# A linear-attention and dense block on one core: 14 additions and two subtractions made by accumulating transfers, query parts in two, and a new order of parts

## The chip, the cores and the metric

The kernel runs on one core of one Trainium2 chip. The metric is the device time of one execution in microseconds. A core has five engines that each take their own instructions in order: TensorE (PE in the profile; its weight loads are PEld), VectorE (DVE), ScalarE (ACT), GpSimd (POOL) and SyncE (SP), which here issues nearly all transfers. Engines wait for each other by semaphores. Transfers run on 16 transfer engines that all queues share.

## The reference

For 2048 tokens `x` of 512 features, a layer norm, a linear attention with 32 heads of 16 features, and a dense pair with Mish between give the output `x + s * g`:

```python
xn = _layernorm(x, axis=-1)
# attention: q, k, v from xn @ wqkv; pq, pk = q, k times w_phi per head
phi_q = jnp.concatenate([_softmax(pq, axis=-1), _softmax(-pq, axis=-1)], axis=-1)
phi_k = jnp.concatenate([_softmax(pk, axis=-1), _softmax(-pk, axis=-1)], axis=-1)
kv = jnp.einsum("bhsf,bhsd->bhfd", phi_k, v)
z  = jnp.einsum("bhsf->bhf", phi_k)
num = jnp.einsum("bhqf,bhfd->bhqd", phi_q, kv)
den = jnp.einsum("bhqf,bhf->bhq", phi_q, z)[..., None] + 1e-6
s = (num / den) @ wo                      # heads side by side
# dense: h = xn @ w1 + b1, mish(h) @ w2
g = _silu(_B_ref(xn, B_w1, B_b1, B_w2))
return x + s * g
```

What the change touches is `z`, the sum of the key maps over all tokens, and `wo`.

## The kernel before

Products keep float32 accuracy by halves: each operand is held as a high half (a rounded copy) and a low half (the value minus the high half), and a product is three matmuls, low x high, high x low and high x high. Large products go by a Strassen-like scheme of seven products of sums instead of eight. So ScalarE makes high halves (`split`, first line), and VectorE or GpSimd the sums and low halves (`either`: whichever the planner picks).

The work is written as some 200 parts, which `ORDER` lists by name, and each part issues operations into a `Program`:

- `wv`, `kh`, `kl`, `kd`, `ks`, `k2`, `k4`, `wq`, `wQ`: loads, sums and halves of the key, value and query weights; `b1` the bias.
- `N0` to `N15` (`norm`): load of 128 tokens, layer norm, transposes, sums and halves of the transposed block.
- `Ka`, `Kb`, `Kc`, `Kd` of token pair c: the seven key and value products of 256 tokens (tiles `kx`, `ky`, `kz`), their evacuation, and `k_soft`, the two softmaxes of a token block into `k0e` to `k15e`. `Kd` has one product, of whose result the map of the even block is made: `Kd6` makes `k12e`.
- `A0` to `A7` (`kv_acc`): the maps of a pair are added to the running sum `zacc` (128 x 1024, 512 KB), and every second time the products `kvp` of maps and values are issued.
- `z` (`sums`): the halves `zacch`, `zaccl` of `zacc`, its product with ones (`pz`), copied into `zb`; the block-diagonal form of `kvp`.
- `Q0` to `Q7` (`q_proj`): seven query products of 256 tokens (`qx`, `qy`, `qz`, six matmuls with 256 columns each) and the query softmaxes; `D0` to `D15` (`den`): the denominators, with `zb`.
- `Fa`, `Fb`, `Fc`, `Fd` of n (`ffn1a` to `ffn1d`): the first dense layer, two products, two, two and one of six matmuls with 512 columns (`fx`, `fy`, `fz`); results are spilled to HBM (`hd`). `P` makes weight halves (`w1ah`, `w1al`, `w1sh`, `w1sl`) and spills them, `M` loads them again (`w1b`).
- `Ua`, `Ub` (`num_a`, `num_b`): numerators; `O` (`att_out`): product with `wo`, spilled. `wo0`, `wo1` (`weights_o`): loads and halves of `wo`.
- `R`, `G` (`ffn2`), `E`, `H`: the second dense layer, SiLU and output.

TensorE executes its products in the order of the list, without exception. All else is ordered by a planner (`Program.simulate`): a list scheduler that plays the program through with a cost per operation (`cost`), a due time per operation that follows from where the TensorE work stands that needs it (changed by the entries of `SHIFT`, "part:operation:nanoseconds"), a pool of tiles, and a model of the transfers. It gives each operation an engine and a place. `locks` keeps VectorE's and GpSimd's operations on SBUF apart in the plan. The engines then run what was planned, each in its order, and wait where data isn't there.

Nearly every instruction is recorded by one line of `issue` (L404 in the profile), so the profile is read by tile names.

Of the kernel before, what the change touches and what calls it, by code (L numbers as in the profile page):

```python
# [48 lines left out]
SHIFT = """
kd:0:-9100 wv1:0:-1100 N1:2:-15000 N1:3:300 N1:5:5800 N1:13:4300 N1:14:-7000 kl:3:-10000 Ka2:3:-9700 N5:6:-2200  # L50
N5:8:-1200 N5:11:13000 N2:0:-3500 N2:2:-2000 N3:4:1500 N3:13:-11400 Kc0:7:4900 Kc0:10:14200 k4:0:-6900 Kd0:6:300
N6:14:-6700 P0:1:4800 P0:5:3800 P0:11:5000 Kb1:3:300 N7:6:-2800 N7:8:7300 N7:9:-6400 N8:8:-2700 N9:13:3600 Kc1:8:1800
Kd1:4:-7300 N10:3:-300 N11:0:5800 P4:0:-7000 P4:4:300 P4:5:3100 N14:8:-6800 Kd3:1:-5000 Kd3:6:-6400 A2:0:-3600
N13:5:-2500 Fa4:1:-1100 Fa4:3:3600 N15:4:10800 N15:6:-5000 N15:11:-300 Kc5:6:4400 Ka6:1:-600 Kc6:5:-300 Kc6:6:2600
P6:6:-1100 P6:8:5100 P3:3:-2600 P3:11:-2000 Kb7:1:2800 Fa3:1:-300 Fa3:3:300 P2:4:-2000 P2:6:1100 P2:10:800 Kd6:6:-8800
Kd6:9:-9500 Fb6:3:-2300 Fc3:1:1600 Fc3:2:800 Fc3:4:7900 wQ:1:2300 wQ:13:6600 Fa2:3:300 Fa2:4:-1900 Fa1:3:900
M4:1:-1400 P5:10:3200 Q0:7:14700 Q0:23:-2000 z:4:1200 z:5:11100 D0:0:800 D0:4:4700 D0:8:-800 L:5:-4200 L:9:-3000
D1:2:-8100 Q1:16:800 Q1:19:300 Q2:3:-15000 Q2:9:-2500 Q2:15:300 Q2:25:-1900 Q3:17:-4300 Q3:18:4700 Fc5:5:9400
D3:7:1800 D4:3:-4000 D4:4:6800 D4:5:1300 D4:6:11900 D4:10:11500 D5:1:-300 Fb11:1:-4700 Q4:7:-600 Q4:16:600 Q4:18:7800
Q4:20:800 Q4:21:-1400 Q4:23:-8800 Q5:25:-600 M3:1:-5000 M3:2:-6700 Fa12:1:800 D6:6:-500 D6:10:300 Fb10:1:-500  # L60
D7:1:5000 D7:4:6600 D8:1:-2400 D8:4:-500 D8:10:1400 Q6:1:4700 D9:10:800 Q7:1:7800 Q7:16:-4700 Q7:20:4800 Q7:21:-13000
Q7:23:-12900 M2:2:-5000 D10:6:-800 M6:2:-4100 D11:1:-1700 Ua0:1:-1100 Ua0:12:-800 Fc9:1:3400 D12:5:-5000 D13:0:-4400
D13:4:12500 Fa13:4:800 Ub0:14:-4300 wo0:1:-4500 Fc13:4:-13100 Fc7:2:15000 R0:8:4700 D14:6:-7800 O3:2:-900 Ua1:2:-4200
Ua1:4:-6700 Ua1:6:-3100 Ua1:11:-5000 Ua1:13:-300 Ua1:14:300 O5:2:-500 Fd13:2:-4200 O6:1:-2200 Ub1:5:-5000 Ub1:6:-2000
Ub1:8:-4500 G7:4:-2000 R2:0:-2200 R1:1:15000 R1:6:4200 R1:10:5800 G8:3:-5000 G8:6:1900 O11:2:-2000 R6:1:4900 R3:2:1600
R3:8:-3300 R4:1:2000 G11:0:-6800 G12:5:3100 G12:6:-1200 G13:5:-1100 G32:3:6500 G34:6:4000 G1:4:-15000 G3:0:5000
G4:0:-4100 G5:5:4000 G35:3:9300 G35:4:-5800 G35:6:3100 G14:0:-10200 G14:3:4000 E0:6:-2600 G15:2:800 G39:6:-300
G16:4:-5000 G41:3:1700 E5:4:-300 G20:0:800 G20:2:-2000 G20:3:-5300 G20:6:-5000 G42:3:5100 G42:5:-300 G43:2:4200
G44:2:300 G44:4:-2000 H4:2:1300 G46:3:6600 G46:6:300 G24:6:500 G47:5:-3000 G26:4:-1600 E6:2:-800 G49:0:-5000
G49:2:4000 G49:6:-1100 G49:9:2000 G49:12:-2200 G49:19:2200 G49:26:5000 G49:31:800 G49:36:2800 G49:42:-4700 G49:43:800  # L70
E7:9:-300 E7:10:15000 H3:7:2300 H6:8:800
"""
ACT_SET = {AF.Exp: 1, AF.Silu: 3, AF.Mish: 2}

# [5 lines left out]
class Program:  # L80
# [141 lines left out]
    def simulate(self, at):  # L222
# [49 lines left out]
        def go(o, e):  # L272
# [124 lines left out]
    def issue(self, tc):  # L397
        first, held = True, None
        for o in self.order():
            for i, (m, a, k) in enumerate(o.impl[o.eng][1]):  # L400

                e = self.eng["A" if first and m == "dma_start" else o.eng]
                first = first and m != "dma_start"
                ins = getattr(e, m)(*a, **k)  # L404
# [47 lines left out]
def block_kernel(ctx: ExitStack, tc: tile.TileContext, x, wqkT, wv, phi, wo, w1, b1, w2, out):  # L452
# [228 lines left out]
    def plus(t, ps):  # L681
        V.tensor_tensor(t, t, ps, op=ALU.add)
# [72 lines left out]
    def kv_d(c):  # L755
# [36 lines left out]
    def kv_acc(p):  # L792
# [379 lines left out]
    def sums():  # L1172
# [20 lines left out]
        for i in range(4):  # L1193
# [46 lines left out]
```

## Time and profile before

| what | value |
|---|---|
| median of 2 runs | 489.16 us (488.93 to 489.39) |
| profiled execution, span from first to last instruction | 488.7 us |
| granted TensorE clock | 1.000 |
| TensorE busy | 480.2 us |
| VectorE, ScalarE, GpSimd busy | 446.2, 293.4, 267.2 us |
| bytes moved by transfers | 105.70 MB, mean 216 GB/s |

The span is what the trace covers; the runs' time has some tenths of a microsecond around it. A busy time counts an engine once, however many of its instructions overlap. The page's rows by slices, each a fortieth of the span (12.2 us), give the busy share in tenths (9 is 90% or more):

```profile
PE   8899999999999999999999999999999999999996
DVE  6999999988899999999999899889989889999894
ACT  3997545654556453635345545677879687777631
POOL 3989998998490446798987686370021024120030
DMA  8812923968867689982959635726465646578172
```

Rows of a transfer give, from left to right, target and source, the issuing queue, the count, KB each and the median time from issue to landing. Rows of a tile give the shortest, median and longest duration in ns, and the first and last start in us. Rows of waits give who waited for whom, the total in us, how often, and the longest.

### The profile page before, as it was taken

To read this page: it belongs to the slowest core of one execution; us is meant where nothing else is said; L and a number is where in the kernel's file an instruction comes from. 1 tells how busy PE (TensorE), PEld (TensorE's weight loads), DVE (VectorE), ACT (ScalarE), POOL (GpSimd) and SP (SyncE) were. 2 spreads that over 40 slices of the span, in tenths; PEclk is the share of its full clock that TensorE was granted. 3 is DMA by queue.
4 is the path that set the end of the run, shared out by engine and by line. 5 is a ranking of instruction groups with operands and counts; after the bars stand their busy time and mean duration, and the time that the engine had idled before them with its cause. 6 is when DMAs were issued, how large, how long until landed. Compare 5 with 4: busy or idle time off the path is not lost.

```text
span 488.7 us, 10325 instructions
## 1 busy us (share of the span) xinstructions
PE 480.2 (98%) x3820; PEld 426.2 (87%) x3820; DVE 446.2 (91%) x893; ACT 293.4 (60%) x453; POOL 267.2 (55%) x197
## 2 busy tenths in 40 slices
PE   8899999999999999999999999999999999999996
PEld 7788888888887889898887878788899999999996
DVE  6999999988899999999999899889989889999894
ACT  3997545654556453635345545677879687777631
POOL 3989998998490446798987686370021024120030
PEclk9999999999999999999999999999999999999999
DMA  8812923968867689982959635726465646578172
GB/s 294 265 48 109 332 99 122 312 197 272 315 217 313 225 301 345 394 300 87 310 199 341 229 115 211 261 85 207 141 193 165 201 154 211 194 234 269 44 250 94
DMA packets 68641, 105.70 MB, mean 216 GB/s; under 512 B 6896, under 2 KB 37744, under 8 KB 68592
## 3 DMA queue, kind: packets, MB, share of 16 engines
q1 hardware_dynamic: 68448, 104.79, 62.9%
q8 instruction: 30, 0.49, 0.4%
q10 hardware_dynamic: 144, 0.26, 0.2%
q14 instruction: 19, 0.16, 0.1%
HBM read 60.60 MB, written 44.43 MB: 215 GB/s over the span
## 4 chain that ended last, share of the span: by engine, by line
PE 81%; DVE 8%; DMA 5%; issue 2%; ACT 1%; SPq 1%; POOL 1%; DVEq 0%; ACTq 0%
PE y L404 20%; PE fx L404 14%; PE pw L404 9%; PE kx L404 7%; PE fy L404 7%; PE qx L404 5%; PE ky L404 3%; PE fz L404 3%; PE qy L404 2%; PE kj L404 2%; PE pn L404 2%; PE kz L404 2%; DVE al L404 2%; DMA wvr<-wv 1%; DMA w1a<-w 1%
## 5 line engine op out<-in xcount | busy, mean ns | idle before, releaser
L404 POOL TENSOR_TENSOR al<-r,ah 128x896 fp32r<-128x896 f32 x8 | 17.0, 2130 | 87.4 <-DMA r<-hd 35.1
L404 ACT ACTIVATE ah<-r 128x896 fp32r<-128x896 f32 x56 | 50.9, 944 | 16.0 <-DVE r L404 12.9
L404 DVE TENSOR_TENSOR al<-r,ah 128x896 fp32r<-128x896 f32 x48 | 54.8, 1171 | 5.0 <-ACT ah L404 3.2
L404 DVE TENSOR_TENSOR r<-r 128x128 f32<-128x128 f32 (+1 forms) x157 | 48.3, 353 | 5.0 <-ACT r L404 3.4
L404 PE MATMUL y<-w2h,al 128*128 128x256 f32 x160 | 45.4, 283 | 0.0
L404 PE MATMUL y<-w2h,ah 128*128 128x256 f32 x160 | 45.3, 283 | 0.0
L404 PE MATMUL y<-w2l,ah 128*128 128x256 f32 x160 | 45.3, 283 | 0.0
L404 PE MATMUL y<-w2t,ah 128*128 128x256 f32 x224 | 41.0, 283 | 0.0
L404 PE MATMUL fx<-fh,w1b 128*128 128x512 f32 x112 | 38.8, 393 | 0.0
L404 ACT ACTIVATE r<-r 128x512 f32<-128x512 f32 x56 | 33.2, 621 | 7.9 <-DMA r<-hd 7.9
L404 PEld LDWEIGHTS y<-w2t,ah 128*128 128x128 f32 x224 | 34.9, 192 | 0.0
L404 PE MATMUL y<-w2t,al 128*128 128x256 f32 x112 | 31.7, 283 | 0.0
L404 PEld LDWEIGHTS y<-w2h,al 128*128 128x128 f32 x160 | 30.7, 192 | 0.6 <-issue 0.4
L404 PEld LDWEIGHTS y<-w2l,ah 128*128 128x128 f32 x160 | 30.7, 192 | 0.2
L404 PEld LDWEIGHTS y<-w2h,ah 128*128 128x128 f32 x160 | 30.7, 192 | 0.0
L404 PE MATMUL y<-w2g,ah 128*128 128x256 f32 x160 | 30.4, 283 | 0.0
L404 PEld LDWEIGHTS fx<-fh,w1b 128*128 128x128 f32 x112 | 21.0, 188 | 5.4 <-issue 1.2
L404 PEld LDWEIGHTS y<-w2g,ah 128*128 128x128 f32 x160 | 25.0, 192 | 0.0
L404 POOL TENSOR_TENSOR r<-r 128x128 f32<-128x128 f32 (+1 forms) x11 | 6.4, 592 | 32.3 <-DMA sr<-so 22.5
L404 PE MATMUL y<-w2g,al 128*128 128x256 f32 x80 | 22.6, 283 | 0.0
L404 ACT ACT_TABLE_LOAD x13 | 16.7, 1283 | 9.2 <-DMA x<-x 4.1
L404 PE MATMUL fx<-fl,w1b 128*128 128x512 f32 x56 | 21.8, 390 | 0.0
(766 smaller groups left out, 1730.0 us busy)
## 6 DMA issues: line engine op xcount, KB each, us to landing
r<-hd SPq DMA_DIRECT2D x56, 256.0 KB, 3.5
xd<-xc SPq DMA_DIRECT2D x8, 896.0 KB, 4.1
w1b<-w1d SPq DMA_DIRECT2D x14, 512.0 KB, 5.5
w1b<-w1d SPq DMA_DIRECT2D x14, 384.0 KB, 4.9
so<-so SPq DMA_DIRECT2D x16, 256.0 KB, 2.1
x<-x SPq DMA_DIRECT2D x15, 256.0 KB, 3.7
w1a<-w SPq DMA_DIRECT2D x7, 512.0 KB, 4.6
w1d<-w1sh SPq DMA_DIRECT2D x7, 512.0 KB, 2.9
```

Source lines behind the costliest of these rows:

```text
L404: ins = getattr(e, m)(*a, **k)
```

## The change

Four things are changed.

1. `kv_acc` no longer adds the maps of pairs 1 to 7 to `zacc` on VectorE or GpSimd. For each of the 14 maps GpSimd issues a transfer from the map's tile to `zacc` that adds to what stands there. The first operation, `k0e` plus `k1e`, stays an addition.
2. `weights_o` makes the low half of `wo` by a ScalarE copy of the high half with the sign turned, and a transfer from GpSimd that adds the loaded weights to it.
3. `q_proj` ends after five of its seven products; the last two, and the softmaxes, are a part of their own, `Qb` (`q_last`).
4. `ORDER` and `SHIFT` are new, and the planner knows the new transfers: a cost on GpSimd, a landing time, and no lock against VectorE.

```diff
+SOFT, SOFTLAT, SOFTRATE = 1000, 2000, 200
...
-Ka6 P6 Ka7 Kb6 Kc6 P3 Fa6 Kb7 Kc7 Fa3 Kd6 A4 P1 Kd7 Fb3 Fb6 Fc3 wQ Fc6 Fd3 P2 A5 A6 Fd6 Fa1 Fa2 Fb1 A7 Fb2 Fc1 Q0 P5
-Fd1 Fc2 z D0 Fa5 D1 M4 Fb5 L Q1 Q2 Fd2 Q3 D2 Fc5 D3 Fa11 M3 D4 D5 Fb11 Fc11 Fd5 Q4 Q5 Fd11 Fa10 Fb10 D6 M5 D7 Fa12
...
+A3 P3 N15 Kd5 P6 Kb6 Kc6 Ka7 Kb7 Kc7 Kd7 Fa3 Fa6 Fb6 Fb3 Kd6 wQ Fc3 Fc6 Fd3 P1 P2 A4 A5 Fa1 Fd6 P5 Fa2 Fb1 Fc1 Fd1
+Q0 Fb2 A6 A7 Fa5 Fb5 Qb0 z Q1 Qb1 Fc2 Fc5 D0 D1 Fd2 Q3 Qb3 Q2 D2 D3 L Qb2 D4 D5 M4 Fa11 Fb11 Q4 Fd5 M3 Fc11 Fd11 Qb4
...
         if e == "Q":
             return 450
+        if m == "dma_start":
+            return SOFT
...
+            if e == "G" and calls[0][0] == "dma_start":
+                dma = max(dma, now + dur + SOFTLAT) + volume(calls[0][1]) / SOFTRATE
+                end = dma
...
-                if i == 0 and o.eng == "G" and held is not None and o.start - held[1] < NEAR:
+                if i == 0 and o.eng == "G" and m != "dma_start" and held is not None and o.start - held[1] < NEAR:
...
     if e == "G":
-        return True
+        return m != "dma_start"
...
+        qs[c] = mm, x, y, p0, p1
+
+    def q_last(c):
+        mm, x, y, p0, p1 = qs.pop(c)
         mm(y, 6, 2, False)
+        a1, b0 = p1[:, 0:2 * P], p0[:, 2 * P:]
         plus(a1, y)
         mm(x, 2, 6, False)
         copy(b0, x)
...
             for e in es:
-                either(zacc, zacc, e, op=ALU.add)
+                G.dma_start(zacc, e, accum_op=ALU.add)
...
     def weights_o(i):
-        w["o"][2 * i:2 * i + 2] = load_pair(wo, "wo", i)
+        raw = load_raw(wo, "wo", i)
+        hi, lo = halves(f"wo{i}", 0)
+        A.activation(hi, raw, AF.Copy)
+        A.activation(lo, f32(hi), AF.Copy, scale=-1.0)
+        G.dma_start(f32(lo), raw, accum_op=ALU.add)
+        w["o"][2 * i:2 * i + 2] = [(hi[:, j, :], lo[:, j, :]) for j in range(2)]
```

Where the sum ends, GpSimd's rows were these before (`w1s1` and `w1al1` are weight sums and a low half of dense block 1; four additions, of k10, k11, k13 and k14, stood on VectorE):

```order
L404 TENSOR_TENSOR k12e_460<-k12e_460,k12r_457 128x1024
L404 TENSOR_TENSOR w1s1_462<-w1s1_462,w1a1_461 128x256
L404 TENSOR_TENSOR zacc_118<-zacc_118,k9e_359 128x1024
L404 TENSOR_TENSOR k15e_451<-k15e_451,k15r_448 128x1024
L404 TENSOR_TENSOR zacc_118<-zacc_118,k12e_460 128x1024
L404 TENSOR_TENSOR zacc_118<-zacc_118,k15e_451 128x1024
L404 TENSOR_TENSOR w1s5_535<-w1s5_535,w1a5_534 128x256
```

And these are GpSimd's rows there now (the line number is that of the changed file; `w1sl5` is a low half of dense block 5, `q1e` the first query map):

```order
L529 DMA zacc_118<-k11e_384 128x1024 [waits DMASW0_49]
L529 TENSOR_TENSOR w1s1_488<-w1a1_487 128x256 [waits DMAHW2_49,PE_49]
L529 TENSOR_TENSOR w1s1_488<-w1a1_487 128x256
L529 TENSOR_TENSOR w1al1_490<-w1a1_487,w1ah1_489 128x768 [waits PE_49,Activation_49]
L529 DMA zacc_118<-k12e_471 128x1024 [waits DMASW1_49,DVE_49,Pool_49]
L529 DMA zacc_118<-k13e_437 128x1024 [waits DMASW2_49]
L529 DMA zacc_118<-k14e_452 128x1024 [waits DMASW3_49]
L529 TENSOR_TENSOR w1s5_513<-w1a5_512 128x256 [waits DMAHW7_49,DMAHW1_49,DVE_49]
L529 TENSOR_TENSOR w1s5_513<-w1a5_512,w1s5_513 128x256 [waits DVE_49]
L529 TENSOR_TENSOR w1sl5_517<-w1s5_513,w1sh5_516 128x1024 [waits DMAHW5_49,PE_49,Activation_49]
L529 DMA zacc_118<-k15e_447 128x1024 [waits DMASW4_49]
L529 TENSOR_TENSOR q1e_548<-q1p_535,q1m_547 128x32x16 [waits DVE_49,Pool_49]
```

All additions now stand in GpSimd's queue, in the order of the maps, and each waits on the semaphore of the transfer before it (the names that begin with DMASW).

On TensorE, `pz` stood between the last of the two products `Fc2` and the first of `Fa5` before:

```order
L404 MATMUL fy2_519<-fl20_108,w1sh2_501 128x512
L404 MATMUL fy2_519<-fh20_107,w1sh2_501 128x512
L404 MATMUL pz0_552<-zaccl_551,oner_85 128x512
L404 MATMUL pz0_552<-zacch_550,oner_85 128x512
L404 MATMUL pz1_553<-zaccl_551,oner_85 128x512
L404 MATMUL pz1_553<-zacch_550,oner_85 128x512
L404 MATMUL fx5_563<-fh00_103,w1al5_537 128x512
```

Now TensorE has it between the last of the two products of `Qb0` and the first of `Q1`:

```order
L529 MATMUL qx0_531<-wq1l_479,fh60_115 128x256
L529 MATMUL qx0_531<-wq1h_478,fh60_115 128x256
L529 MATMUL pz0_558<-zaccl_557,oner_85 128x512
L529 MATMUL pz0_558<-zacch_556,oner_85 128x512
L529 MATMUL pz1_559<-zaccl_557,oner_85 128x512
L529 MATMUL pz1_559<-zacch_556,oner_85 128x512
L529 MATMUL qx1_562<-wqh0_476,fl00_104 128x256
```

The four products of `Fa5` and `Fb5` have moved ahead of `pz`, and the two of `Fc2` behind it. TensorE's list has the same matmuls in all, 2677 rows in both.

More of the change, by code (lines that the diff above doesn't have):

```diff
@@ L53 @@
[L53 to L67, printed above, removed]
@@ new lines @@
+Kc7:9:-700 Kc7:11:1300 Kd7:1:-100 Kd7:2:13200 Kd7:3:1700 Kd7:4:-4000 Kd7:5:200 Kd7:6:7700 Kd7:7:14900 Kd7:8:1000
+Kd7:9:600 Fa3:1:300 Fa3:3:6000 Fa3:4:-5600 Fa6:1:-300 Fa6:3:-300 Fa6:4:-9500 Fb3:3:-4100 Kd6:1:500 Kd6:2:400
+Kd6:3:-9800 Kd6:4:-6100 Kd6:5:-2600 Kd6:6:-6600 Kd6:7:1600 Kd6:8:-6000 Kd6:9:-9300 wQ:1:1600 wQ:6:400 wQ:8:2000
+wQ:9:2600 wQ:10:500 wQ:11:-1200 wQ:12:300 wQ:13:-800 Fc3:2:15000 Fc3:4:9700 Fc6:2:500 Fc6:4:800 Fc6:5:-2500
+Fd3:1:3900 Fd3:2:-2100 P1:0:-6200 P1:1:-500 P1:2:8800 P1:3:-1300 P1:4:2800 P1:5:2900 P1:6:1700 P1:9:-300 P1:11:100
@@ new lines @@
+P2:0:500 P2:1:-2600 P2:3:7000 P2:4:-1200 P2:5:-800 P2:7:-700 P2:8:300 P2:9:-1700 P2:10:-100 P2:11:4800 A4:0:-500
+A4:1:1800 A5:0:2100 A5:1:100 Fa1:3:-200 Fd6:1:100 Fd6:2:2000 P5:0:-1000 P5:1:14800 P5:2:-300 P5:3:-600 P5:4:-700
+P5:5:-2500 P5:8:-1500 P5:9:100 P5:10:5700 P5:11:-400 P5:12:1200 Fa2:1:200 Fa2:3:1600 Fb1:1:1000 Fb1:3:900 Fc1:1:1300
+Fc1:2:8000 Fc1:5:-700 Fd1:2:700 Q0:1:-13900 Q0:3:1200 Q0:7:-1200 Fb2:1:100 A6:0:-2000 A6:1:400 A7:1:-9400 Fa5:1:2700
+Fa5:3:1000 Fa5:4:2300 Fb5:1:9400 Fb5:3:-300 Qb0:1:-6800 Qb0:3:-15000 Qb0:6:-15000 Qb0:7:3600 Qb0:8:5000 Qb0:9:700
@@ new lines @@
+Qb0:10:3300 Qb0:11:-400 Qb0:12:-100 Qb0:13:-400 z:0:-9100 z:1:2200 z:2:10100 z:3:10200 z:4:-7500 z:5:-3400 z:6:9900
+z:8:-2200 z:10:-3300 z:13:-400 z:14:3100 z:15:-3200 Q1:1:1300 Q1:3:9700 Q1:5:-8600 Q1:7:-4200 Qb1:1:4700 Qb1:3:400
+Qb1:5:-2100 Qb1:6:1700 Qb1:7:-400 Qb1:8:400 Qb1:9:-100 Qb1:10:2300 Qb1:12:-500 Qb1:13:12000 Qb1:15:3600 Fc2:1:900
+Fc2:4:15000 Fc2:5:9900 Fc5:1:-3000 Fc5:4:-13700 Fc5:5:15000 D0:0:100 D0:1:-8500 D0:3:700 D0:4:4700 D0:5:-1100
+D0:8:300 D0:9:-1000 D0:10:-600 D1:1:-500 D1:2:1200 D1:4:8300 D1:5:100 D1:6:-200 D1:7:-2100 D1:8:800 D1:9:-300
@@ new lines @@
+D1:10:300 Fd2:1:10800 Fd2:2:-300 Q3:1:4300 Q3:5:9300 Q3:7:-500 Q3:9:-3000 Qb3:1:-15000 Qb3:5:-1100 Qb3:8:12400
+Qb3:11:-1200 Qb3:12:400 Qb3:13:-200 Qb3:15:100 Q2:1:4200 Q2:3:14300 Q2:5:-700 Q2:7:5500 Q2:9:1600 D2:0:600
+D2:1:-6000 D2:2:1800 D2:3:2500 D2:5:-13900 D2:6:100 D2:8:300 D2:9:100 D2:10:-300 D3:3:300 D3:4:1800 D3:5:300
+D3:6:2200 D3:7:6200 D3:8:-200 D3:10:900 L:0:-12300 L:1:400 L:2:500 L:5:-3100 L:6:-400 L:9:200 L:10:-3100 L:11:200
+L:12:-2000 L:13:-800 Qb2:1:-14500 Qb2:3:-200 Qb2:5:1800 Qb2:6:-200 Qb2:7:4700 Qb2:8:-200 Qb2:9:2700 Qb2:10:-400
@@ new lines @@
+Ub0:13:2200 Ub0:14:-3500 Ub0:15:-1800 Ub0:16:2700 Fb13:1:1800 Fb13:3:-2000 D13:0:400 D13:1:6200 D13:2:-10500
+D13:3:6100 D13:4:400 D13:5:1700 D13:7:400 D13:8:-600 D13:9:500 D13:10:1000 wo1:0:400 wo1:1:-300 wo1:2:-700
+wo1:3:-12500 Fc13:1:-7000 Fc13:2:15000 Fc13:4:2000 Fc13:5:5000 O3:1:5200 O3:2:6900 O5:1:-7000 D14:1:-2400 D14:2:-500
+D14:3:2800 D14:5:-500 D14:6:-8300 D14:8:300 D14:9:200 D14:10:-1200 R5:0:1900 R5:1:-800 R5:2:-10000 R5:3:-8900
+R5:5:-4400 R5:6:8600 R5:7:-3200 R5:8:100 O7:2:3800 O4:1:-500 O4:2:1700 D15:0:12900 D15:1:-2800 D15:2:-200
@@ new lines @@
+O6:2:2700 O2:1:-200 O10:1:600 O14:1:-7000 O14:2:500 O11:1:-6700 O11:2:-2100 R0:1:4900 R0:2:15000 R0:3:2000
+R0:4:-5500 R0:5:300 R0:6:-300 R0:7:-3400 R0:8:-2600 R0:9:3300 R0:10:9000 O15:1:-7000 O15:2:3600 O8:1:-1700 O8:2:-400
+O13:1:-1300 O13:2:15000 O9:1:-15000 R1:1:13300 R1:2:-1600 R1:4:-4900 R1:6:3100 R1:7:6000 R1:8:-8700 R1:9:1200
+R1:10:4700 O12:2:8200 R3:0:-8200 R3:1:1200 R3:3:-400 R3:4:-200 R3:5:1900 R3:6:2900 R3:7:400 R3:8:-100 R3:9:800
+R3:10:-600 G7:1:-5200 G7:2:-5100 G7:3:-100 G7:4:-10200 R6:0:-800 R6:1:-100 R6:2:-600 R6:3:-2800 R6:6:-14200
@@ new lines @@
+G14:0:400 G14:1:2200 G14:3:-300 G14:4:300 G14:5:1100 G14:6:3700 G15:0:-2200 G15:1:600 G15:2:12300 G15:3:3400
+G15:4:1800 G15:5:-800 G15:6:-9300 G16:0:400 G16:1:-200 G16:2:200 G16:4:2100 G16:5:-900 G16:6:2600 G17:0:-4500
+G17:2:600 G17:4:11200 G17:5:-1900 G17:6:1800 G18:0:-14800 G18:1:-9000 G18:2:300 G18:3:-6300 G18:4:8500 G18:5:100
+E0:0:-400 E0:1:5200 E0:2:13900 E0:3:-400 E0:4:-15000 E0:6:-13000 E4:0:1200 E4:1:9200 E4:3:-100 E4:4:-600 E4:5:-600
+E4:6:-14200 G19:0:300 G19:1:-6300 G19:2:-800 G19:3:-13700 G19:4:-1300 G19:5:-11600 G19:6:-1100 G20:0:2700
@@ new lines @@
+E6:1:14000 E6:3:800 E6:4:-1000 E6:5:-6200 E6:6:8400 G49:1:-1200 G49:3:100 G49:4:400 G49:5:-1300 G49:6:1300
+G49:7:-200 G49:9:-10400 G49:11:-100 G49:12:-2200 G49:15:400 G49:16:-800 G49:18:1400 G49:19:1100 G49:20:-300
+G49:22:700 G49:24:-1000 G49:25:700 G49:26:14100 G49:27:-200 G49:28:-400 G49:31:1400 G49:32:-2200 G49:33:-300
+G49:36:4200 G49:37:100 G49:41:-1500 G49:42:-4700 G49:43:2400 G49:44:-100 G49:45:200 G49:46:-3100 G49:47:100
+G49:48:8100 G49:55:-1300 E7:0:1800 E7:2:700 E7:3:1200 E7:4:6500 E7:5:200 E7:6:-13500 E7:7:-2000 E7:8:300 E7:9:5500
@@ L762, in kv_d @@
         k_soft(2 * c, k0, x)
+    qs = {}
     def q_proj(c):
```

124 lines of the change are left out of this document (109 added, 15 removed).

## The prediction, before the result was known

> **What bounds the kernel now.** I read the page's busy shares first, then the busy time by stretches, then what TensorE waited for, then the chain that ended last. The first row has a count and a busy time for each engine:
>
> ```profile
> span 488.7 us, 10325 instructions
> PE 480.2 (98%) x3820; PEld 426.2 (87%) x3820; DVE 446.2 (91%) x893; ACT 293.4 (60%) x453; POOL 267.2 (55%) x197
> ```
>
> TensorE has something in flight nearly always. Where it has not shows the table of busy times in five stretches (the last columns are the granted clock, the busy share of the transfer engines and GB/s):
>
> ```profile
> 0.00:20.00 20.00, 16.38 (x107) 14.52 (x107) 15.04 (x44) 11.58 (x23) 12.21 (x18) 1.00 0.87 287
> 20.00:140.00 120.00, 120.00 (x799) 99.73 (x799) 109.84 (x210) 76.12 (x120) 106.01 (x78) 1.00 0.59 201
> 140.00:160.00 20.00, 19.73 (x325) 15.96 (x324) 19.97 (x27) 12.15 (x17) 6.00 (x4) 1.00 0.78 286
> 160.00:480.00 320.00, 320.00 (x2563) 292.10 (x2562) 297.33 (x605) 192.47 (x293) 142.93 (x99) 1.00 0.64 217
> 480.00:488.70 8.70, 4.13 (x35) 3.93 (x33) 3.98 (x10) 1.10 (x3) 0.00 (x0) 1.00 0.22 77
> ```
>
> TensorE is idle 3.62 us in the first 20 us, 0.27 us between 140 and 160, and 4.57 us at the end, after its last matmul: 8.46 us in all, at a full clock throughout. Its own waits say the same:
>
> ```profile
> PE wake L404 <- DVE mhalf L527: 1.1, 1, 1.1
> PE wkf L404 <- DMA wkT<-wqkT: 1.0, 2, 0.7
> PE wqf L404 <- ACT wqf L404: 0.7, 1, 0.7
> PE pt L404 <- DVE x L404: 0.6, 2, 0.4
> PE fx L404 <- DVE w1al L404: 0.3, 1, 0.3
> PE kz L404 <- POOL wv1l L404: 0.2, 1, 0.2
> ```
>
> After the start it waits once, 0.3 us, for a half of a dense weight. A busy TensorE could still be a slow one, so the chain is read for the pace of a product of six matmuls with 512 columns, and of the last long stretch:
>
> ```profile
> 13.60 2.41 POOL wv1l L404
> 124.20 6.44 DMA w1a<-w
> 159.40 1.36 PE fy L404 x6
> 355.62 85.45 PE y L404 x712
> ```
>
> 1.36 us for six is 0.227 us each, and 85.45 us for 712 is 0.120 us each, for half the columns: both kinds run at one pace, and the sum of such products fills the span. So the kernel is bound by TensorE's work. The change keeps every matmul, so only the 8.46 us can be won, 1.7% of the span, and of these neither the 1.1 us before the first matmul nor the 4.57 us behind the last is touched: the four last outputs keep their steps. What is left to win is at most 8.46 - 1.1 - 4.57 = 2.8 us. What can be lost has no such bound: TensorE takes its work in a fixed order, and a late operand stops all that stands behind it.
>
> **The change, part by part.** *Sums of key maps.* The running sum `zacc` loses 14 additions on GpSimd and VectorE and gets 14 accumulating transfers:
>
> ```profile
> 60.00:170.00 110.00, 4.86 (x4) 0.31 (x1) 26.45 (x11) 1.00 0.67 231
> L404 POOL TENSOR_TENSOR zacc<-zacc,k15e x1: 2400/2400/2400, 167.3 to 167.3; 128x1024 f32<-128x1024 f32 x1
> L404 PE MATMUL pz<-zaccl,oner x2: 392/394/396, 172.6 to 173.1; 128*128 128x512 f32 x2
> L404 POOL TENSOR_TENSOR k12e<-k12e,k12r x1: 1936/1936/1936, 139.1 to 139.1; 128x1024 f32<-128x1024 f32 x1
> 128.32 0.39 PE L404 MATMUL kx<-wkh,xc 128*128 128x512 f32 x1
> 6.33 0.56 POOL L404 TENSOR_TENSOR rs<-rs,mhalf 128x1 f32<-128x1 f32 x1
> ```
>
> The first row is the tile `zacc` alone: GpSimd has 11 operations (the first one, of `k0e` and `k1e`, stays), so ten times 2.40 us = 24.0 us go from it, and four operations, 4.86 us, from VectorE. In their place GpSimd issues 14 transfers. No row shows what an issue from GpSimd costs: between nothing and the 2.40 us of the addition that it replaces. I take 0.6 us, by the row that is nearest, a GpSimd operation on one element in a partition (0.56 us): 8.4 us. Both engines get lighter; none of that is on TensorE's path, so it is worth 0 by itself.
>
> What the sum does set is the moment at which `pz`, its product with ones, can run. Each transfer waits for the one ahead, and GpSimd stands still meanwhile. The last block of keys to be ready is `k12e`. Before, its product began at 128.32 and its scaling ended at 139.11 + 1.94 = 141.05, 12.7 us later. The new list of parts puts five products of 1.36 us ahead of it that stood behind it before (one of `Kd7`, two each of `Fb6` and `Fb3`), so it begins at 135.1, and `k12e` is ready at 147.8. From there k12, k13, k14 and k15 are added one after another: 4X, where X is one transfer from issue to landing. Then come the two halves of `zacc`; from the end of the last addition (169.66) to `pz` (172.6) these took 2.9 us. `pz` itself moves back: four products of block 5 (`Fa5`, `Fb5`) are put ahead of it and two of block 2 (`Fc2`) behind it, so its turn comes at 172.6 + 2 x 1.36 = 175.3. It is not late while 147.8 + 4X + 2.9 <= 175.3, so X <= 6.1 us, and each further microsecond of X stops TensorE for 4 us.
>
> X has no row. It moves 512 KB, and adds. The rows for such sizes (KB each, median us from issue to landing), and the load of the transfer engines where `w1b` is read:
>
> ```profile
> wqd<-wqf SPq DMA_DIRECT2D x2, 512.0 KB, 2.7
> w1d<-w1sl SPq DMA_DIRECT2D x7, 512.0 KB, 4.2
> w1a<-w SPq DMA_DIRECT2D x7, 512.0 KB, 4.6
> w1b<-w1d SPq DMA_DIRECT2D x14, 512.0 KB, 5.5
> 180.00:200.00 20.00, 20.00 (x144) 18.82 (x143) 18.85 (x42) 7.11 (x15) 13.64 (x12) 1.00 0.96 353
> 115.00:175.00 60.00, 59.73 (x519) 49.57 (x518) 57.03 (x86) 31.70 (x46) 29.61 (x21) 1.00 0.76 271
> ```
>
> The lower end is 2.7 us, a plain write of this size. The upper end is a read and a write in turn, 4.6 + 4.2 = 8.8 us. I take 5.5 us: it is twice the plain 2.7 for a transfer that reads two things, and what such a load takes where the engines are fuller than here (0.96 against 0.76). Then `pz` can run at 147.8 + 22.0 + 2.9 = 172.7, 2.6 us before its turn: cost 0. At 2.7 it is 0 as well; at 8.8 it is 147.8 + 35.2 + 2.9 - 175.3 = 10.6 us.
>
> The Trainium skill ("DMA: Bandwidth & Descriptors", section "Anatomy of one DMA — SWDGE (gpsimd) path") gives for a transfer issued from GpSimd about 2.0 us plus its bytes at 436 GB/s, the fixed part mostly the wait for the last byte to be confirmed. By that formula, an estimate for a plain copy, 512 KB take 3.2 us, four in turn 12.8 us, and the cost is 0 too; but in a chain in which each waits for the one before, the fixed part is paid 14 times and never overlapped, which speaks against this change. No transfer of the trace is issued from GpSimd, so it can't be compared with a row here.
>
> *What is queued behind.* GpSimd issues k12, k13 and k14 in a row, so it stands for 2X = 11 us. Behind them is the low half `w1sl5`, done at about 147.8 + 11 + 0.6 + 2 x 0.74 + 2.4 = 163.3; TensorE wants it two products of 1.36 us and two of six matmuls with 256 columns (0.72 us) ahead of `pz`, at 175.3 - 4.2 = 171.1: hidden by 7.8 us. `zacch` on ScalarE and `zaccl` on VectorE also have work behind them, evacuations of block 2 and the query softmax; if the sum is late, they are too, but TensorE then stands at `pz` anyway.
>
> *Output weights.* `wo` loses two GpSimd subtractions of 2.4 us and gets two ScalarE copies and two transfers. The chain shows how late they are wanted:
>
> ```profile
> 290.90 5.44 PE pw L404 x24
> ```
>
> That is 118 us behind `pz`; with either end of X it is hidden: 0.
>
> *Query parts in two.* `Qb` is the last two products of a query block as a part of its own, so other products may stand between. No instruction more: 0.
>
> *New order.* At the start, `wv1l` on GpSimd ends at 13.60 + 2.41 = 16.0, TensorE goes on with it at once, and its place is kept: six matmuls come first in both orders. Its load moves behind one of 256 KB; and the `wqf` wait of 0.7 us comes later. I put the start at 0, between -0.7 (that wait goes) and +0.7 (one more like it). The wait of 0.3 us for `w1al` goes with the changed order: -0.3, or 0 if the like half, which GpSimd now makes behind the transfer of k11, is as late.
>
> The sum: 488.7 - 0.3 + 0 + 0 = 488.4 us of span. The profile gives no time of its own run beside that span; the median of the two runs, 489.16, lies 0.46 above it, and with that 488.9 us is predicted.
>
> **The rivals.** *The sum comes late.* X is over 6.1 us. For it: the upper row sum of 8.8, and no row for an adding transfer. Against it: most rows of the size are under 6. X = 7.3 gives 4.8 us, 493.7; X = 8.8 gives 10.6 us, 499.5. From X = 8.6 on it is over 2% slower. This is the case on the other side.
>
> *The transfer engines fill up.* From 115 to 175 they are busy 0.76 of the time at 271 GB/s, so 512 KB cost 524 / (271 / 0.76) = 1.47 us of all sixteen. Some seven of the adds fall there: 10.3 us if each counts once, 20.6 if twice, against 0.24 x 60 = 14.4 us to spare. At twice the share would be 1.10, and a load of `w1a` (6.44 us in the chain) 0.7 us longer; three such loads are on the way to TensorE, 2 us: 490.9. The Trainium skill (same page, section "Issuing engines are not separate DMA queues") says that transfers from all issuing engines run on the same sixteen, so a second queue brings no bandwidth; the trace with its one large queue can't show it.
>
> *The start and the small waits all go.* All 2.8 us that can be won: 486.4, -0.6%. Against it: the start is held by weight loads and GpSimd's two low halves, which stay.
>
> *Nothing of it is felt*, since the additions were hidden anyway: 489.2, within the forecast.
>
> **How the numbers follow.** Forecast, no stall over 1.5 us: 0.66. The sum late by less than 2%: 0.10, by more: 0.07. Full transfer engines: 0.14, nearly all within 2%, 0.01 beyond with the late sum on top. The full win of the start: 0.03. A gain over 2% is excluded by the 2.8 us, but for an error in what I take for TensorE's work: 0.01 is left for it, taken from the last case. About 2% is what a measurement of this kernel can tell from no change. So faster 0.01, same 0.91, slower 0.08. The low end, 487.2, is 488.9 with the start at -0.7 and another 1 us of the small waits; the high end, 494.0, is X = 7.3, and leaves out some 0.13 of the late cases.
>
> **What would show it.** Right: TensorE busy 480 us again, no wait for `zacch` or `zaccl`, 14 transfers of `zacc` with 4 to 6 us to landing, GpSimd's busy time down by some 20 us. Wrong: a wait of `pz` of several us, behind transfers of 7 us and more; waits of `fx` for `w1al` or `w1sl` made by GpSimd (GpSimd kept by its transfers), or behind `w1a` loads (full transfer engines). The forecast is wrong as a whole if TensorE's matmuls take other times than before.

## The result, and the profile after

The changed kernel takes **510.74 us** (median of two runs, 510.25 to 511.22), against 489.16 before: a ratio of 1.0441, 95% interval 1.0424 to 1.0458. That is 21.6 us slower, where no change was predicted and 494.0 was the high end. One execution of e1 below, 542.58 us at a granted clock of 0.842, was in a slower state and is left out of that run's time.

The page of the changed kernel (busy time, share of the span and instructions of each engine; then the queue of GpSimd's transfers with packets, MB and share of the sixteen transfer engines):

```profile
span 508.5 us, 10325 instructions
...
PE 486.9 (96%) x3820; PEld 427.8 (84%) x3820; DVE 446.4 (88%) x899; ACT 286.9 (56%) x439; POOL 256.5 (50%) x207
...
q0 software_dynamic: 2304, 8.39, 8.4%
```

The same 3820 matmuls, and TensorE no longer fills the span. Of the 19.8 us that the span grew, 13.1 are idle time of TensorE and 6.7 are busy time, with the same matmuls. The profiled run took 510.25 us, 1.75 more than its span. What TensorE waited for (us in all, times, longest):

```profile
PE pz L529 <- DVE zaccl L529: 3.9, 1, 3.9
PE y L529 <- DVE al L529: 2.4, 3, 1.0
PE pn L529 <- DVE ph L529: 1.8, 1, 1.8
PE pw L529 <- issue: 1.5, 1, 1.5
PE kj L529 <- DVE xl L529: 1.3, 1, 1.3
PE wake L529 <- DVE mhalf L652: 1.1, 1, 1.1
PE kx L529 <- POOL xc L529: 1.1, 1, 1.1
PE fx L529 <- POOL w1al L529: 0.9, 1, 0.9
PE fx L529 <- POOL w1sl L529: 0.9, 1, 0.9
```

Before, one wait of 0.3 us was left after the start. Now there is a large one at `pz` and many of about a microsecond, some of them hundreds of microseconds behind the last transfer of `zacc`. First the large one. Here are GpSimd's rows in time where the chain of additions ends (start, us, what; in brackets the idle time before and what ended it) and the row of VectorE that makes `k12e` ready; then two rows on the tile `zacc` and the last four transfers (us from issue to landing at the end); then two stretches of all engines as in the prediction's table (the granted clock ahead of the last two columns).

```profile
151.66 0.87 POOL L529 DMA_DIRECT2D zacc<-k12e  x1 [2.11 <-DVE w1s L529]
160.24 0.87 POOL L529 DMA_DIRECT2D zacc<-k13e  x1 [7.71 <-DMA zacc<-k12e]
...
174.04 0.86 POOL L529 DMA_DIRECT2D zacc<-k15e  x1
```

```profile
147.50 3.15 DVE L529 TENSOR_TENSOR k12e<-k12e,k12r 128x1024 f32<-128x1024 f32 x1
```

```profile
L529 ACT ACTIVATE zacch<-zacc x1: 1056/1056/1056, 182.0 to 182.0; 128x1024 fp32r<-128x1024 f32 x1
...
DMA to landing us min/median/max: 4.6/6.9/9.7
```

```profile
zacc<-k12e POOLq DMA_DIRECT2D x1, 512.0 KB, 8.2
zacc<-k13e POOLq DMA_DIRECT2D x1, 512.0 KB, 7.0
zacc<-k14e POOLq DMA_DIRECT2D x1, 512.0 KB, 4.7
zacc<-k15e POOLq DMA_DIRECT2D x1, 512.0 KB, 7.9
```

```profile
180.00:184.00 4.00, 0.52 (x5) 0.31 (x3) 0.90 (x1) 1.91 (x3) 0.00 (x0) 1.00 1.13 398
184.00:188.00 4.00, 3.62 (x13) 3.24 (x14) 3.12 (x6) 1.52 (x3) 2.47 (x3) 0.57 0.74 228
```

The last four additions take 182.0 - 151.7 = 30.3 us: 27.8 us of transfers and 2.5 us between them, most of it 1.7 us before `k15e`, whose issue stands on GpSimd behind a low half (`w1sl`). While the chain ends and the sum is split, TensorE has 0.5 us of work in four, and in the four after that its clock is granted at 0.57. By single microseconds the clock is 0.75 from 184, 0.50 from 185 and from 186, 0.54 from 187 and 1.00 from 188: so 2 x 0.43 x 4 = 3.4 us ran at half, and 1.7 us of work were lost on top of the wait. Together 5.6 us; 16 us were still to be found.

### The profile page after: what moved, and what is told of

The parts are those of the page before. It is cut to its first block, busy times and chain, and to the rows that moved or that the text cites. A ratio compares the mean times of both kernels' runs of the same rounds, so it can differ in the third digit from the quotient of the medians.

```text
span 508.5 us, 10325 instructions
## 1 busy us (share of the span) xinstructions
PE 486.9 (96%) x3820; PEld 427.8 (84%) x3820; DVE 446.4 (88%) x899; ACT 286.9 (56%) x439; POOL 256.5 (50%) x207
## 3 DMA queue, kind: packets, MB, share of 16 engines
q0 software_dynamic: 2304, 8.39, 8.4%
## 4 chain that ended last, share of the span: by engine, by line
PE 60%; DMA 11%; DVE 10%; POOL 7%; issue 6%; ACT 3%; SPq 2%; POOLq 0%; DVEq 0%; ACTq 0%
PE y L529 15%; PE fx L529 10%; PE pw L529 7%; PE kx L529 6%; PE fy L529 5%; DMA r<-hd 4%; PE qx L529 3%; PE ky L529 3%; POOL ez L529 2%; PE kj L529 2%; PE fz L529 2%; SPq L529 2%; DVE al L529 2%; PE pn L529 2%; DMA zacc<-k12e 2%
## 5 line engine op out<-in xcount | busy, mean ns | idle before, releaser
L529 POOL TENSOR_TENSOR r<-r 128x128 f32<-128x128 f32 (+1 forms) x16 | 9.0, 566 | 125.0 <-DVE r L529 89.4
L529 DVE TENSOR_TENSOR r<-r 128x128 f32<-128x128 f32 (+1 forms) x152 | 44.3, 334 | 8.4 <-ACT r L529 7.4
L529 PEld LDWEIGHTS y<-w2t,al 128*128 128x128 f32 x112 | 21.5, 192 | 0.9 <-DVE al L529 0.9
L529 DVE TENSOR_REDUCE tz<-ez 128x64 f32<-128x1024 f32 x16 | 19.3, 1209 | 2.0 <-POOL ez L529 2.0
```

## Experiments

The theories at the start: **T**, the transfers themselves make the loss (late landings, GpSimd standing, load on the transfer engines); **O**, the new order of parts makes it. Ratios are against the kernel before on the same chip. A list of parts and its table of shifts go together; where a kernel is "planned again", the planner also gives engines and places anew.

### Either half of the change without the other

The first pair keeps every instruction of the changed kernel where it stands and makes only its transfers additions again (e2: those of `zacc` alone).

```
+ if GpSimd's instruction is a transfer (e2: into zacc):
+     GpSimd.tensor_tensor(d, d, source, op=add)
- G.dma_start(d, source, accum_op=ALU.add)
```

> The changed kernel with every engine's instructions in the same order, but each of the 16 adding transfers replaced, at its place in GpSimd's queue, by the addition itself (about 2.4 us on GpSimd instead of an issue of 0.9 us and a landing after 6.9 us). Theory T (the adding transfers land too late, and GpSimd stands still for them): the four last additions take 9.6 us instead of 28, pz is in time, 487 to 494 us. Theory O (the new order is bad by itself, the transfers are hidden): 505 us or more.

> The same, but only the 14 transfers of zacc are replaced by additions in place; the two of the output weights stay. Theory T with the zacc chain as the whole cause: within 1 us of the run with all 16 replaced. If the output weights' transfers have a share (pw waited 1.5 us in the changed kernel, behind a 512 KB transfer that landed after 8.3 us): 1.5 to 4 us above it. Theory O: 505 us or more.

The second pair is planned again: e3 has the new lists (`ORDER`, `SHIFT`, `Qb`) with `either(zacc, zacc, e)` and `load_pair(wo)`, e4 the old lists with transfers for `zacc` and the planner's costs of them.

> New order and query parts in two, but the sums and the output weights made as before, and planned anew by the planner. Theory T: 487 to 494 us. Theory O: over 500 us. Here the planner may put instructions elsewhere, so it tells less than the run with the order kept.

> The kernel before, old order and undivided query parts, with the 14 transfers of zacc alone, planned with the change's costs for them. Theory T: as slow as the changed kernel, 500 to 520 us, with pz waiting for the sum. Theory O: 487 to 492 us.

Measured: e1 523.07 us (1.0701, 1.0659 to 1.0743), e2 523.96 (1.0694, 1.0633 to 1.0755), e3 527.72 (1.0793, 1.0758 to 1.0828), e4 509.05 (1.0419, 1.0399 to 1.0438). Putting additions back makes the new order worse, and the transfers alone cost the old order as much as the whole change. As the whole cause, O falls with e4; T would fall with e1 and e3, but e1 and e2 turn out below to carry a cost of their own, so that T falls as the whole cause only with e11. A new theory, **R**, came of it: a list of parts with its shifts fits one set of durations, and whatever differs from it pays in many places. TensorE's two longest waits in e3:

```profile
PE pt L529 <- ACT x L529: 7.2, 1, 7.2
PE fx L529 <- DVE w1sl L529: 6.6, 1, 6.6
```

### The old plan with transfers, and with nothing else changed

No list and no plan changes in e5 and e9: the additions are exchanged for transfers when the instructions are written out, all 14 in e5, `k2e` to `k9e` in e9. In e7 the only edit is an empty `SHIFT`.

```
+ if m == "tensor_tensor" and out is zacc and in0 is zacc:      # e9: and in1 is k2e..k9e
+     G.dma_start(zacc, in1, accum_op=ALU.add)
```

> The kernel before, with its own order, table of shifts and plan of every engine left as they are; only the 14 additions into zacc are issued as accumulating transfers from GpSimd, at the place where each addition stood (the four of VectorE's at that place in the order of the whole program). wo, the query parts and the list of parts are the old ones, and nothing is planned again. Theory T (the transfers cost the time by themselves: each takes 5 to 10 us to land, GpSimd stands at the next one, and other transfers get slower): 500 to 515 us, with k10 to k15 one behind the other, pz waiting several us, and fx waiting for low halves from GpSimd. Theory R (it is the new plan, not the transfers, that is bad: each table of parts and shifts fits one set of durations, and any other plan loses 15 to 20 us): under 495 us, the only wait that of pz.

> The kernel before, its own order and plan; only the eight additions of k2e to k9e are issued as transfers, at the places where the additions stood on GpSimd. k10e to k15e are added as before. Theory T (only the serial end of the chain hurts; transfers that have time to land are hidden): 487.5 to 489.5 us, the same as before or up to 1 us faster, with no new wait of TensorE. Theory F (transfers slow the loads beside them: 0.82 of the transfer engines busy between 60 and 100 us instead of 0.57): 491 us or more, with waits of fx for w1a or w1sl between 80 and 150 us.

> The kernel before with its table of shifts emptied and planned again; list of parts, additions and wo are the old ones, no transfer from GpSimd. Theory R (the tables are fitted to one chip's durations, and a plan that is not fitted loses 15 to 20 us through many small waits): 500 to 515 us, with waits of fx and pt spread over the first 200 us. Theory T (the transfers alone make the loss): 489 to 494 us.

Measured: e5 510.24 us (1.0419, 1.0400 to 1.0439), e9 489.59 (1.0002, 0.9993 to 1.0011), e7 510.88 (1.0441, 1.0426 to 1.0457). The waits of e5 and all those of e9 (the last four rows):

```profile
PE pz L409 <- DVE zaccl L409: 8.0, 1, 8.0
PE fx L409 <- DVE w1sl L409: 7.6, 1, 7.6
```

```profile
PE wake L409 <- DVE mhalf L532: 1.1, 1, 1.1
PE wqf L409 <- ACT wqf L409: 0.7, 1, 0.7
PE wkf L409 <- DMA wkT<-wqkT: 0.4, 1, 0.4
PE pt L409 <- DVE x L409: 0.4, 1, 0.4
```

e9 against e5 is the clearest pair: in one plan the eight early transfers are free and the six late ones cost 20 us. Two rows of stretches of e9 show that it is not their load, and the median of its landings is the 5.5 us that I had taken for X:

```profile
60.00:100.00 40.00, 40.00 (x306) 33.23 (x305) 35.88 (x75) 22.79 (x34) 30.94 (x24) 1.00 0.82 228
100.00:140.00 40.00, 40.00 (x297) 32.74 (x296) 36.16 (x58) 21.84 (x30) 27.99 (x22) 1.00 0.94 294
```

```profile
DMA to landing us min/median/max: 4.4/5.5/7.2
```

The transfer engines are 0.94 busy and TensorE misses nothing. In e5 GpSimd stands at each of the late ones; its first and its last:

```profile
148.63 0.89 POOL L405 DMA_DIRECT2D zacc<-k10e  x1 [4.70 <-DMA zacc<-k9e]
...
183.15 0.86 POOL L405 DMA_DIRECT2D zacc<-k15e  x1 [4.72 <-DMA hd<-hb]
```

From 148.6 the six take until past 183; the six additions of the kernel before ran from 157.1 to 169.7, four of them on VectorE in 1.2 us each. e7 shows what the fit is worth: without its table of shifts the old list, with no transfer at all, is 4.4% slower. e9 bounds R: eight operations of other durations, in a plan made for the old ones, cost nothing.

### Parts of the changed kernel

e6 and e8 exchange transfers for GpSimd additions in place, as e2 does: e6 those of `k12e` to `k15e`, e8 the two of `wo`.

> The changed kernel in its own order, only k12e to k15e added by GpSimd at the places where their transfers stood (2.4 us each); k2e to k11e stay transfers. Theory T1 (the late end of the chain is the main cost: 3.9 us of waiting at pz and what the halved clock and the late D blocks add behind it): 497 to 503 us. Theory T2 (pz is one wait of many; the rest comes from transfers that slow the others and from GpSimd's standing all along): 504 to 508 us, pz without a wait, and nearly all of the other waits as in the changed kernel.

> The changed kernel in its own order, only the two low halves of the output weights made by an addition on GpSimd instead of a transfer, at the place where the transfer was issued; the 14 transfers of zacc stay. If the two transfers of wo cost what pw waited for in the changed kernel (1.5 us): 509 us. If they are hidden as predicted: 510.5 to 511. If GpSimd's 2 x 2.4 us more work there is late in its turn: 512 to 514.

Measured: e6 511.45 us (1.0441, 1.0408 to 1.0475), e8 511.36 (1.0456, 1.0414 to 1.0498). `wo` makes no difference that shows within the 2 us of e8's interval. In e6 the wait of `pz` is gone and another has come:

```profile
PE fx L532 <- DVE w1al L532: 3.8, 1, 3.8
```

The same half of a weight on VectorE, first in the changed kernel, then in e6, where GpSimd adds `k12e` (from 151.53) and `k13e` (from 154.15) beside it:

```profile
152.44 0.94 DVE L529 TENSOR_TENSOR w1al<-w1a,w1ah 128x768 fp32r<-128x768 f32 x1
```

```profile
154.55 3.09 DVE L532 TENSOR_TENSOR w1al<-w1a,w1ah 128x768 fp32r<-128x768 f32 x1
```

0.94 us became 3.09. The plan of the kernel before keeps such pairs of VectorE and GpSimd apart (`locks`); an addition put where none was planned does not. So e6 met neither theory's time and could not divide the loss, and e1 and e2 are burdened in the same way. (The changed kernel has one such pair too: the 3.15 us for `k12e` above stood beside a GpSimd subtraction; the like operation of `k9e` took VectorE 1.22 us.) The next ones therefore take transfers out instead of exchanging them, and divide the lists at `wo1`: what stands up to there is called the head, the rest the tail. TensorE's products in the head stand as in the kernel that gives it:

```
e10  changed kernel, k10e..k15e not issued
e11  changed kernel, no transfer into zacc issued
e12  changed kernel; ORDER and SHIFT of before behind wo1
e13  e12 without any transfer into zacc
e14  e12 with k2e..k9e only
e16  kernel before; ORDER and SHIFT of the changed one behind wo1
```

> The changed kernel in its own order; the six transfers of k10e to k15e are not issued, so the sum of the key maps lacks these six blocks. k2e to k9e are still transferred. Theory T (the late chain, GpSimd's standing at it and the halved clock are what the transfers cost): 501 to 504 us, 6.8 us at pz and its clock and some 1 us of waits around it less than the changed kernel's 510.7. Theory F (the transfers' load on the transfer engines, early ones included): over 505 us.

> The changed kernel in its own order; none of the 14 transfers of zacc is issued, so the sum has only the blocks k0 and k1; wo's two transfers stay. What is left over the 489.2 us of before is the cost of the new order by itself. Theory T (all comes from the transfers): 487 to 490 us. Theory O (the new order has a loss of its own behind 270 us, where no transfer of zacc runs: waits for ph, wo1 and al, 7.5 us by the progress of TensorE): 494 to 499 us.

> The changed kernel with its list of parts and shifts up to wo1, and behind that the list and the shifts of the kernel before (planned again; TensorE's products are the same in both up to there). Theory O (the new order's tail costs 7.5 us by itself): 502 to 504.5 us, and from 290 us on TensorE falls back no further. Theory T (the tail's waits are a result of the late head, or of wo's transfers): 509 to 512 us. A third way, that any list that was not fitted costs more: over 514 us.

> As e12 (new list and shifts up to wo1, old ones behind), with none of the 14 transfers of zacc issued: the sum has only the blocks k0 and k1. If the new order's loss sits in its tail alone: 488 to 491 us, TensorE's progress within 1 us of before all along. If the new head loses too: 493 to 496 us, with waits of fx or kx before 270 us.

> As e13, but k2e to k9e are transferred; only k10e to k15e are left out of the sum. If the early transfers cost through GpSimd's standing (kx waits for xc, 1.3 to 1.9 us, made behind the wait for k7e's landing): 1.5 to 3 us more than e13. If that was an effect of the tail or of scatter: the same as e13 within 1 us.

> The kernel before up to wo1, and behind it the new list's parts and shifts (planned again; no transfers, zacc and wo as before). If the new tail is bad by itself: 494 to 498 us, with the waits of pn for ph, of pw and of y for al that the changed kernel has. If those waits came from the late head or from wo's transfers: 489 to 491 us.

| kernel | head | transfers of zacc | tail | us | ratio (95%) |
|---|---|---|---|---|---|
| e13 | new | none | old | 494.6 | 1.0103 (1.0081 to 1.0124) |
| e14 | new | early 8 | old | 497.23 | 1.0165 (1.0150 to 1.0180) |
| e12 | new | all 14 | old | 505.62 | 1.0323 (1.0298 to 1.0349) |
| changed | new | all 14 | new | 510.74 | 1.0441 (1.0424 to 1.0458) |
| e10 | new | early 8 | new | 501.85 | 1.0249 (1.0222 to 1.0277) |
| e11 | new | none | new | 498.97 | 1.0203 (1.0163 to 1.0243) |
| e16 | old | none | new | 498.27 | 1.0192 (1.0173 to 1.0210) |

Runs of these kernels scatter by 1 to 5 us (e11 from 497.3 to 502.7), those of before by one. Read down the first four rows, each step times 489.2 us: the new head by itself 5.0 us, the early transfers 3.0, the late six 7.7, the new tail 5.8; 21.6 in all. By the next two rows the early eight cost 2.3, the late six 9.4 and the tail 4.9. By the intervals a step of the first four rows is good to some 1.5 us, one that uses e11 to some 2.4. "New head" is the list with its shifts, `Qb` and `wo`'s two transfers together; and e11 and e13 also leave out the additions that the kernel before makes, so what they lose is lost with less work. The new order without any transfer into `zacc` is e11, 2.0% slower. e10, e11, e13 and e14 came within the times of one of their theories, e12 1.1 and e16 0.3 us above.

e16's tail costs more, 9.4, and its list differs there in one point: between the second and the third block of `pn` it has only the two dense products of `Fc13` where the changed kernel has those of `Fb13` too. That is 2.7 us less work there, its wait for `ph` is 4.4 us instead of 1.8, and the clock behind it is granted at 0.66 from 308 to 312, where the changed kernel keeps 1.00 behind its wait. That this is the whole difference is not shown.

What each part waits for, one or two rows of e14, e13 and e16:

```profile
PE kx L383 <- POOL xc L383: 2.1, 1, 2.1
```

```profile
PE fx L383 <- DMA w1b<-w1d: 1.1, 2, 0.9
PE kj L383 <- DVE xl L383: 0.9, 1, 0.9
```

```profile
PE pn L375 <- DVE ph L375: 4.4, 1, 4.4
```

The rows of e13 show only a part of what its head loses. Behind the first 20 us TensorE is idle 2.7 us more than before (1.5 us between 200 and 260, where it was not idle), and it is busy 2.7 us more with the same matmuls (482.9 us against 480.2, at a clock of 0.998; 1.0 us of it in the thirty `wake` matmuls of the start). A matmul of 512 columns is in flight for 0.39 us and the next starts 0.227 us later, so a stop of less than 0.16 us does not show as idle; that such stops are the rest is not shown.

**The early transfers** cost mainly through one place. GpSimd's rows of the changed kernel, and of e9, where the same transfers were free:

```profile
114.35 0.87 POOL L529 DMA_DIRECT2D zacc<-k8e  x1 [2.06 <-DMA zacc<-k7e]
...
116.36 2.65 POOL L529 TENSOR_TENSOR xc<-xs,xc 128x1024 fp32r<-128x1024 f32 x1
```

```profile
112.92 2.42 POOL L409 TENSOR_TENSOR xc<-xs,xc 128x1024 fp32r<-128x1024 f32 x1
...
119.55 0.86 POOL L405 DMA_DIRECT2D zacc<-k8e  x1
```

In the new order the transfer of `k8e` stands ahead of `xc`; GpSimd stands 2.06 us for `k7e` to land, and the `kx` that needs `xc` is late. In the old order `xc` comes first. The same rule made the wait of 0.9 us for `w1al` in the changed kernel: GpSimd makes that half behind the transfer of `k11e`, for which it stood 2.2 us until `k10e` had landed; e11 and e13 have no such wait. **The tail**: the new list has four output products between the second and the third block of `pn` where the old one had seven,

```
before:  ... Ub0 Fc7 D13 R1 Fc13 O1 O3 Fd13 R0 O4 D14 O5 O0 O2 D15 O7 Ua1
after:   ... Ub0 Fb13 D13 wo1 Fc13 O3 O5 D14 R5 O7 O4 D15 Ub1
```

and in the trace 48 matmuls of `pw` instead of 84, so 36 x 0.227 = 8.2 us less of TensorE's work under which VectorE makes `ph`, and one dense product of 1.36 us less. TensorE waits for `ph` there in the changed kernel, e2, e6, e10, e11 and e16 (1.7 to 4.4 us), and not in e12, e13 and e14 with the old tail. In e1, e3 and e8 it has the new tail and comes late enough not to wait. The wait of `pw` in the changed kernel, 1.5 us put down to "issue", is also gone with the old tail; the trace names no cause for it.

One more moves `pz` alone: in e12's list `z Q1 Qb1 Fc2 Fc5 D0` becomes `Q1 Qb1 Fc2 Fc5 z D0`, planned again.

> As e12 with all 14 transfers, but the part z (zacch, zaccl, pz) stands behind Q1, Qb1, Fc2 and Fc5 instead of ahead of them, some 12 us of products later (planned again). If the late six cost by pz's place alone: no wait for zaccl, no stretch at half clock, so 4.3 + 2 to 3 us less than e12's 505.6, that is 498 to 500 us. If they cost through GpSimd's standing or the dense weights' loads: 503 to 506 us. If the query blocks' denominators now come late instead: a wait of fx or qx behind 200 us and over 503 us.

Measured: 532.6 us (1.0885, 1.0849 to 1.0922). The signs of its third way are there, waits of `fx` and `qx` behind 200 us and more than 503 us. The longest waits are these:

```profile
PE fx L381 <- DVE hc L381: 11.6, 2, 9.7
PE fx L381 <- ACT ha L381: 8.4, 1, 8.4
```

The 8.4 us come at 186, from ScalarE:

```profile
184.62 1.06 ACT L381 ACTIVATE zacch<-zacc 128x1024 fp32r<-128x1024 f32 x1 [9.25 <-DMA zacc<-k15e]
185.58 0.67 ACT L381 ACTIVATE ha<-fx,b1t 128x512 f32<-128x512 f32 x1
```

The new plan puts the half of the sum ahead of an evacuation that TensorE needs. ScalarE stands 9.25 us for the last transfer, and the late chain is paid there although `pz` has moved away. The 9.7 us come at 309, for an evacuation that VectorE makes behind 12 us of work without a pause, most of it on query maps and denominators. So e15 is in keeping with R, and leaves untried whether `pz` could be moved without upsetting the plan. No version was faster than the kernel before.

## Why the prediction was wrong

**What bounds it** held: TensorE's work is the same, and a late operand stops all behind it. The fault is in which operands I asked about. Two steps failed, with about half of the 21.6 us each (9.9 us are left in e11, without any transfer into `zacc`): the term of the new order, which I put at nothing, and the chain of transfers with what stands behind it, which I put at nothing too.

**"New order. At the start the cost is 0, between -0.7 and +0.7".** The start did cost nothing (TensorE is idle 2.7 us in the first 20, 3.6 before). But the new lists cost 5.0 us in their head and 5 to 6 in their tail without any transfer of `zacc`. I read the new order at its start and around `pz`, and took every other place for covered without a reason. The tail's loss could have been read from the two lists: four output products between two blocks of `pn` instead of seven, in a kernel whose VectorE is 91% busy. Of the head's 5.0 us the waits of a microsecond or less are shown with their places; they are about half of it, and why the fitted list keeps clear of them stays open.

**"Then `pz` can run at 147.8 + 22.0 + 2.9 = 172.7, 2.6 us before its turn: cost 0".** The mechanism was right and its sizes were off. `k12e` was ready at 147.5 + 3.15 = 150.7, since TensorE began its product at 138.5 and not at 135.1, and its transfer was issued at 151.7: 3.9 us late. Four transfers took 27.8 us, not 22.0: 5.8 more. The 2.5 us between them I had not counted, and the halves took 2.4 us, 0.5 less than I had. So `pz` ran at 184.4, 11.7 us after 172.7. It waited only 3.9 us because TensorE itself came to it at 180.5, 5.2 us after the predicted turn: 11.7 - 2.6 - 5.2 = 3.9. In e13, without the chain, it came at 175.7, 0.4 us off the predicted turn. The rival "the sum comes late" named the mechanism; that its 4.8 us (4.6 by its own formula) lie near the 3.9 is luck, two errors that nearly cancel. And the price of a wait is more than its length: the late six cost 7.7 to 9.4 us, with the clock and smaller waits. The low half `w1sl` behind `k14e` was done at 171.72 + 2.38 = 174.1, 10.8 us later than I had it, and in time for TensorE at 176.2 only because that was late too. The prediction's estimate of 3.2 us for a plain copy of this size lies below each of the fourteen (4.6 to 9.7 us).

**"What is queued behind"** looked at `k12e` to `k14e` only. The rule was there (GpSimd stands until the transfer ahead has landed) and was not asked of the transfers before: 2.3 to 3.0 us, most of it at `xc`. The wait for `w1al`, which the sum took at -0.3 or 0, became 0.9 by that rule.

**"The transfer engines fill up"** was the wrong worry by itself: e9 runs at 0.94 without a new wait. Whether the second queue's 8.39 MB slow others in the changed kernel is not shown: two 512 KB reads of `wqd` took 8.4 us to landing, 4.6 before, but 6.7 in e13 without any transfer into `zacc`.

**GpSimd's relief** was over-rated, and worth nothing, as predicted: its busy time fell by 10.7 us, not 20, and e9, with 12.0 us less, takes the same time as before. One issue took 0.86 to 1.17 us where I took 0.6. **`wo`** cost nothing that shows (e8). **`Qb`** was not tried alone.

**The sum's last term**, 0.46 us around the span, was a difference of two runs: the profiled runs of the changed kernel and of the experiments take 1.7 to 2.0 us more than their spans, not some tenths. **"TensorE busy 480 us again"**, the sign of being right, failed as well: 486.9 us. **The range** ended where the one late wait I had thought of ended; a change that rewrites a whole order has more places to be late than one.

## What to carry

Where work is ordered by fitted tables, a rewritten order is a change of its own and has to be read at every place where one engine hands over to another, by counting the work that covers each hand-over; with the shifts emptied, the old order alone lost 4.4%. A chain of transfers that each wait for the last is free as long as nothing with a due time stands behind one on the issuing queue, or behind its sum on an engine that reads it, and dear at its end, where each link is paid in full: eight early links cost nothing in one order, 3 us in another, and six late ones 8 to 20. Taking the suspected work out divides a loss more cleanly than putting the old work back.

## What was not expected of the hardware

An idle TensorE can lose more than the idle time. In the changed kernel the clock was granted at 0.57 in the stretch behind the wait of 3.9 us. Here is e6 in the stretch behind its 3.8 us, and then, at one and the same place of the list, e8 behind a wait of 2.26 us (which ended at 119.6) and e6 behind one of 2.37 us (at 119.1), both for `xc`:

```profile
156.00:160.00 4.00, 2.31 (x6) 1.83 (x7) 4.00 (x2) 0.00 (x0) 3.77 (x2) 0.50 0.39 157
```

```profile
121.00:124.00 3.00, 3.00 (x9) 2.32 (x8) 3.00 (x7) 1.54 (x2) 2.19 (x3) 0.50 0.55 109
```

```profile
119.00:125.00 6.00, 5.79 (x24) 4.48 (x25) 5.84 (x11) 3.20 (x4) 3.71 (x4) 1.00 0.64 147
```

So a wait of little more than 2 us can halve the clock or leave it: in these runs the length alone does not decide. In e8 the clock fell more than a microsecond after the work had gone on. The Trainium skill ("TensorE: Matmul & The Clock Gate", section "Part 1: The HAM clock gate (the "warmup" mystery)") says that the clock has two states, half and full, and comes back after a busy window of about 3.4 us. The 3.4 us of the changed kernel agree; in e6 the clock came back 5.1 us after the wait had ended.

An addition on GpSimd slows VectorE beside it: in e6 0.94 us became 3.09 for one 128x768 subtraction, and the three additions beside VectorE's work took 2.5 to 3.0 us instead of 2.40. And an adding transfer holds the transfer engines longer than its size tells: the packets of 16 of them took 8.4% of the span, so 0.084 x 508.5 / 16 = 2.7 us of all sixteen for each 512 KB, where the prediction's rate for the other transfers gave 1.47.
